# FNet with a gated MLP: MLP blocks of seven units, the first product copied inside PSUM, and x by features for the second half

## The chip, the cores and the metric

The kernel runs on one core of a Trainium2 chip. The metric is the device time of one execution in microseconds (us). Of the kernel before, three runs are given: 821.25, 821.55 and 821.78 us, median 821.55. The engines are named as in the profile: PE (TensorE, matmuls), DVE (VectorE), ACT (ScalarE), POOL (GpSimd) and SP (SyncE, which here issues loads); PEld is PE's loading of weights.

## The reference

The input x has 2048 rows (positions) of 512 features, in float32. What is computed, cut to what matters:

```python
xn = layernorm(x)                                   # over the 512 features
a = einsum("bsd,ed->bse", xn, dft_hid_re)           # 512 x 512
b = einsum("bsd,ed->bse", xn, dft_hid_im)
s = einsum("ts,bse->bte", dft_seq_re, a) - einsum("ts,bse->bte", dft_seq_im, b)   # 2048 x 2048
g = xn @ w_gate                                     # 512 x 1792
u = xn @ w_up
g = silu((sigmoid(g) * u) @ w_down)                 # 1792 x 512
return x + s * g
```

## The kernel before, in words

**Arithmetic.** Every float32 product is made of three matmuls at the lower-precision float32 format of PE: each operand is split into a high part (an ACT copy, line 67) and a low part (a DVE subtraction, line 68), and `mm3` (lines 70 to 73) adds high by high, high by low and low by high into one PSUM bank. On top of that each 2x2 block product is made with seven products instead of eight, so that operands are sums of blocks (`combine`, line 119, on DVE; `x_sum`, line 216, for x) and outputs are sums of products, partly added in PSUM.

**Phases.** (1) `start` opens with the MLP block h=0, g=0 (h: half of the positions, 1024 each; g: one of seven groups of 256 hidden features). There x arrives in tiles of 128 positions, is normalised (`norm_a`, `norm_b`), transposed on PE (`turn`, line 177) and copied out of PSUM (`keep_hi` line 196, `keep_lo` line 202, `keep_raw` line 188); its matmuls (line 555) are 256 columns wide. (2) The blocks h=0, g=1 to 6 and h=1, g=0 come from `block_units`, and h=1, g=1 to 6 from `late_units`. (3) `seq_units` makes the transform over positions: four blocks of positions (`tc_`), seven products, four parts (`pp`) each. (4) `hidden_units` makes the transform over features, multiplies by the gate and writes out.

**An MLP block.** Seven products k of two outputs (gate and up), each of 12 matmuls of 512 columns, gather in three pairs of banks: `ga`/`ua`, `gb`/`ub`, `gc`/`uc`. The order is 1, 2, 6, 5, 7, 4, 3. Product 1 goes to the a banks; `snap` copies it into a page on ACT (line 309 in `block_units`, 473 in `late_units`). Product 2 goes to the b banks, and `plus` adds them to that page on DVE (line 313, 477). Product 6 goes on in the a banks, is snapped, and so on until product 4. The second product of a block's result (`down`, four items of 12 matmuls; in the second half the class `Seven`, seven items of 6) is carried out within the next block. In the first half these items are units of their own:

```python
add(xo(1, 2) + wo(1, 2), u1)
add(bw, lambda: carried(0, 1, 0, 0))
add(xo(6, 5) + wo(6, 5), u3)
add(bw, lambda: carried(1))
```

`gather` (lines 292 to 296) copies their two banks into a page and POOL stores it to `g_part`, adding onto what is there.

**What sets the order.** Nothing is planned by costs. The program is a list `units` of (needs, run), walked at the end; each engine executes in the order in which the program issues. At unit n the walk first runs the hooks that `sooner(n, ...)` left, then issues loads for the units up to n+5, then makes the splits for the units up to n+2, then runs the unit, then runs the hooks of `after(n, ...)`:

```python
for k in range(n, min(n + SPLIT_AHEAD + 1, len(units))):
    for p in units[k][0]:
        p.get()
run()
```

Loads are issued on SP's queue, stores on POOL's; a load waits for the store that it reads. Working memory is 53 pages of 128 x 1024 float32. In `start`, the weights of the first four products of the next block are split while the opening block runs (`units[0 if n < 2 else 2][0][2 + n % 2].get()`: products 1, 2, 6, 5). The outputs of the opening block pass `gated` (line 566 sigmoid on ACT, 567 product on DVE) and `finish` (lines 274 and 275, the split), and after the last of them `x_sum(h, 1)` and `x_sum(h, 2)` are issued.

**Side work** in the h=0 blocks: the tiles 8 to 15 of x (the second half) are fetched, normalised, transposed in four groups of two tiles (eight transposes each) and stored; sums of the transform's operands are made ahead and stored (`t_part`, `s_part`); the sums and splits of x for h=1 are placed around the border of the halves, some before and some after it.

Of the kernel before, what the change touches and what calls it, by code (L numbers as in the profile page):

```python
# [15 lines left out]
P = 128  # L16
# [7 lines left out]
SB = 512  # L24
# [8 lines left out]
def fnet_glu_kernel(ctx: ExitStack, tc: tile.TileContext, x, x_t, c_re, c_im, w_h, w_gu, w_down, out):  # L33
# [22 lines left out]
    nc.scalar.activation(warm, mhalf, AF.Sigmoid)  # L56
    xn_part = dram.tile([2, 2, 2, P, 4, D // 2], F32, name="xn_part")
# [6 lines left out]
    t_part = dram.tile([2, 4, P, 2, SB], F32, name="t_part")  # L64
# [87 lines left out]
    def norm_a(i):  # L152
        st = stat.tile([P, 6], F32, name="st")
        mv = stat.tile([P, 2], F32, name="mv")
        rs = stat.tile([P, 2], F32, name="rs")
        nc.vector.bn_stats(st, xs[i])
        nc.vector.bn_aggr(mv, st)
        nc.gpsimd.tensor_scalar(rs[:, 0:1], mv[:, 1:2], EPS, None, op0=ALU.add)
        nc.gpsimd.tensor_tensor(rs[:, 1:2], rs[:, 0:1], mhalf, op=ALU.pow)
        st_of[i] = mv, rs  # L160

    def norm_b(i):
        mv, rs = st_of.pop(i)
        nc.vector.tensor_scalar(xs[i], xs[i], mv[:, 0:1], rs[:, 1:2], op0=ALU.subtract, op1=ALU.mult)
# [106 lines left out]
    def finish(h, hs, b, f, s):  # L271
        pg = page([2, SB])
        hs[f, b] = pg[:, 0, :], pg[:, 1, :]
        nc.scalar.activation(pg[:, 0, :], s, AF.Copy)
        return lambda: nc.vector.tensor_sub(pg[:, 1, :], s, pg[:, 0, :].bitcast(F32))

    def down(job, n):

        h, g, hs, wd = job
        b, i = divmod(n, 2)  # L280
        for o in range(2):
            at = slice((2 * i + o) * P, (2 * i + o + 1) * P)
            po = bank("pd")
            for f in range(2):
                mm3(po, [t[:, at] for t in wd[f].get()], hs[f, b], f == 0, f == 1)
            yield (2 * h + b) * 2 + i, po

# [10 lines left out]
    def block_units(h, g, before, late, keep=None):  # L298

        w = w_operands(h, g)  # L300
        hs, s, ps = {}, {} if keep is None else keep.s, {}
        wdl = Load(w_down[g], [2, D])
        wd = [Parts([wdl], lambda f=f: wdl.load()[:, f, :], [D], joint=True) for f in range(2)]
        job = (h, g, hs, wd)

        def snap(k, tag):
            s[k] = page([2, SB], F32)
            for m, c in enumerate("gu"):
                nc.scalar.activation(s[k][:, m, :], ps[c + tag], AF.Copy)  # L309

        def plus(k, tag):
            for m, c in enumerate("gu"):
                nc.vector.tensor_add(s[k][:, m, :], s[k][:, m, :], ps[c + tag])
            nc.scalar.activation(s[k][:, 0, :], s[k][:, 0, :], AF.Sigmoid)

        def go(k, tag, first=False):
            for m, c in enumerate("gu"):
                if first:
                    ps[c + tag] = bank(c + tag)
                product(k, ps[c + tag], w, h, m, first)  # L320

        def carried(n, k=None, b=0, f=0):
            outs = list(down(before, n)) if before else []
            if k is not None:
                nc.vector.tensor_mul(s[k][:, 0, :], s[k][:, 0, :], s[k][:, 1, :])
            if outs:
                gather(before[1], outs)
            if k is not None and keep is None:
                finish(h, hs, b, f, s[k][:, 0, :])()

        def u1():
            go(1, "a", True)
            snap(1, "a")
            go(2, "b", True)
            plus(1, "b")

        def u3():
            go(6, "a")
            snap(2, "a")
            go(5, "c", True)  # L340

        def u5():
            go(7, "a")
            snap(3, "a")
            plus(3, "c")

        def u7():
            go(4, "a")
            s[4] = page([2, SB], F32)
            nc.scalar.activation(s[4][:, 0, :], ps["ga"], AF.Sigmoid)  # L350

        def u8():
            go(3, "c")
            nc.vector.tensor_mul(s[4][:, 0, :], s[4][:, 0, :], ps["ua"])
            late = finish(h, hs, 0, 1, s[4][:, 0, :]) if keep is None else lambda: None
            plus(2, "c")
            late()

        n = len(units)
        for i, v in zip((-2, -1, 1, 4), w["s"]):  # L360
            sooner(n + i, v.get)
        if h == 0:
            for i in range(2):
                after(n + 5 * i, lambda i=i: nc.gpsimd.dma_start(ws_part[g, i], w["kept"][i].get()))
        bw = list(before[3]) if before else []
        xo = lambda *k: [xop[h, n] for n in k]
        wo = lambda *k: [w[n] for n in k]
        add(xo(1, 2) + wo(1, 2), u1)
        add(bw, lambda: carried(0, 1, 0, 0))
        if late:  # L370
            add(*late.pop(0))
        add(xo(6, 5) + wo(6, 5), u3)
        if late:
            add(*late.pop(0))
        add(bw, lambda: carried(1))
        add(xo(7) + wo(7), u5)
        add(bw, lambda: carried(2, 3, 1, 1))
        add(xo(4) + wo(4), u7)
        add(xo(3) + wo(3), u8)
        add(bw, lambda: carried(3, 2, 1, 0))  # L380
        if keep:
            keep.spread(len(units) - 7)
        return keep or job


    SEVEN = (2, 1, 6, 7, 4, 5, 3)
    waiting = []

    class Seven:


        def __init__(self, g):
# [71 lines left out]
    def late_units(h, g, before):  # L464

        w = w_operands(h, g)
        job = Seven(g)
        s, ps = job.s, {}
        n = len(units)
        def snap(k, tag):  # L470
            s[k] = page([2, SB], F32)
            for m, c in enumerate("gu"):
                nc.scalar.activation(s[k][:, m, :], ps[c + tag], AF.Copy)

        def plus(k, tag):
            for m, c in enumerate("gu"):
                nc.vector.tensor_add(s[k][:, m, :], s[k][:, m, :], ps[c + tag])

        def gate(k):
            nc.scalar.activation(s[k][:, 0, :], s[k][:, 0, :], AF.Sigmoid)  # L480

        def times(k):
            nc.vector.tensor_mul(s[k][:, 0, :], s[k][:, 0, :], s[k][:, 1, :])

        def last():
            s[4] = page([2, SB], F32)
            nc.scalar.activation(s[4][:, 0, :], ps["ga"], AF.Sigmoid)

        tail = {
            1: lambda: snap(1, "a"),  # L490
            2: lambda: plus(1, "b"),
            6: lambda: snap(2, "a"),
            7: lambda: (snap(3, "a"), plus(3, "c")),
            4: last,
            3: lambda: plus(2, "c"),
        }
        gated = {2: 1, 7: 3, 3: 2}
        CH = {1: "a", 2: "b", 6: "a", 5: "c", 7: "a", 4: "a", 3: "c"}

        def unit(k, d):  # L500
            first = k in (1, 2, 5)
            for m, c in enumerate("gu"):
                tag = c + CH[k]
                if first:
                    ps[tag] = bank(tag)
                product(k, ps[tag], w, h, m, first)
            if k in tail:
                tail[k]()
            if d:
                d[0].run(d[1])  # L510
            if k in gated:
                gate(gated[k])
            if k == 4:
                nc.vector.tensor_mul(s[4][:, 0, :], s[4][:, 0, :], ps["ua"])
# [12 lines left out]
    def start(h, g):  # L527
# [4 lines left out]
        w, hs, ps = {}, {}, {}  # L532
# [11 lines left out]
        def chunk(q, f, order, between=None):  # L544
# [5 lines left out]
            for n, (u, v) in enumerate(order):  # L550
                if n and n - 1 in (between or {}):
                    between[n - 1]()
                for j, m, k in itertools.product(range(2), repeat=3):
# [5 lines left out]
                        start=n == d == 0,  # L559
# [4 lines left out]
        def gated(b, f):  # L564
# [3 lines left out]
            return lambda: finish(h, hs, b, f, s)()  # L568

        def begin():  # L570
# [27 lines left out]
            for p in units[0][0] + units[2][0]:  # L598
                p.load()
# [27 lines left out]
            for q in range(4):  # L627
                for f in range(2):
# [11 lines left out]
                    if 0 <= n < 4:  # L640
                        units[0 if n < 2 else 2][0][2 + n % 2].get()
# [6 lines left out]
        return (h, g, hs, wd), begin  # L648
# [30 lines left out]
    def sums_ahead(n, make, blocks, to, at=(3, 5, 6, 8)):  # L679
# [7 lines left out]
        for i, v in enumerate(blocks):  # L687
            sooner(n + i // 2, v.load)
        for i, v in enumerate(steps):
            after(n + at[i], lambda v=v: step(*v))  # L690
# [36 lines left out]
    def seq_units(job):  # L727
# [8 lines left out]
        for tc_ in range(NT):  # L736
            n = len(units)
            if tc_ == 1:
                blocks = [Load(w_h[i, j], [4, D // 2]) for i in range(2) for j in range(2)]
                sums_ahead(n + 6, diffs, blocks, w_part, (3, 4, 5, 6))  # L740
# [102 lines left out]
            for k in ORDER:  # L843
                for pp in range(4):
                    m = len(units)
                    if (tc_ or pp > 1) and k in bop["t", pp]:
# [115 lines left out]
    with tc.manual_schedule():  # L962
# [3 lines left out]
        for h in range(NH):  # L966
            n = len(units)
            for g in range(NG):
                m = len(units)
                if h and g:  # L970
                    job = late_units(h, g, job)
# [91 lines left out]
```

## Time and profile before

| what | value |
|---|---|
| median of the three runs | 821.55 us |
| the profiled execution's own time | 821.45 us |
| its span (first to last instruction) | 819.7 us |
| mean granted clock of PE | 0.999 |
| PE busy | 810.4 us, 99% |
| DVE busy | 644.7 us, 79% |
| ACT busy | 490.9 us, 60% |
| POOL busy | 144.3 us, 18% |
| HBM traffic | 122.16 MB read, 88.08 MB written |

A group row of the profile reads: line, engine, operation, out<-in by the program's names, out<-in as partitions x elements and type, x count | busy us, mean ns of one | idle time of the engine just before them, and what ended most of it. A row of the timeline reads: start in us from the start of the span, duration, engine, line, operation, out<-in, count, and in brackets the idle time before it and what ended it. A row of the waits reads: engine, what waited, <- what it waited for: us in total, times, longest. A row of the chain reads: start, duration, engine, tile, line, count. "PE ga L71" is the first matmul of `mm3` into the bank `ga`.

### The profile page before, as it was taken

How to read it: one execution, taken by the hardware profiler on the slowest of the kernel's cores; microseconds unless marked ns; L12 is line 12 of the kernel's file. 1: busy time of each engine (PE TensorE's matmuls, PEld its weight loads, DVE VectorE, ACT ScalarE, POOL GpSimd, SP SyncE). 2: the span in 40 equal slices, each digit the busy share in tenths (PEclk: the TensorE clock that was granted, in tenths of full speed). 3: DMA queues.
4: the chain of work that ended last, by engine and by line, in shares of the span. 5: the costliest groups of instructions: out<-in, count | busy, mean ns of one | idle time of the engine just before them, and what ended most of it. 6: DMA issues, size and time to landing. Idle time of an engine off the chain costs nothing.

```text
span 819.7 us, 10476 instructions
## 1 busy us (share of the span) xinstructions
PE 810.4 (99%) x3686; PEld 672.9 (82%) x3686; DVE 644.7 (79%) x816; ACT 490.9 (60%) x762; POOL 144.3 (18%) x214
## 2 busy tenths in 40 slices
PE   8999999999999999999999999999999999999997
PEld 7988888888878888888888888888888888888786
DVE  6798867757788867876797796889888976997956
ACT  4566655655677888887787773444354545535441
POOL 3143432321111122222121100011101110002201
PEclk9999999999999999999999999999999999999999
DMA  8459999799667889989999997358937994789984
GB/s 289 174 176 407 265 267 267 188 320 311 162 170 172 231 177 215 250 203 197 281 292 306 278 336 271 137 203 313 323 136 282 353 384 147 254 317 399 331 254 78
DMA packets 59253, 207.27 MB, mean 253 GB/s; under 512 B 6592, under 2 KB 6848, under 8 KB 59200
## 3 DMA queue, kind: packets, MB, share of 16 engines
q0 software_dynamic: 25072, 87.57, 42.4%
q1 hardware_dynamic: 34128, 119.03, 40.0%
q8 instruction: 29, 0.48, 0.2%
q14 instruction: 24, 0.20, 0.1%
HBM read 122.16 MB, written 88.08 MB: 256 GB/s over the span
## 4 chain that ended last, share of the span: by engine, by line
PE 93%; DVE 3%; ACT 1%; issue 1%; DMA 0%; POOL 0%; SPq 0%; DVEq 0%
PE pd L71 6%; PE pd L72 6%; PE pd L73 6%; PE ga L71 5%; PE ga L72 5%; PE ua L72 5%; PE ga L73 5%; PE ua L71 5%; PE ua L73 5%; PE uc L71 3%; PE gc L72 3%; PE uc L72 3%; PE gc L73 3%; PE gc L71 3%; PE uc L73 3%; PE gb L72 3%
## 5 line engine op out<-in xcount | busy, mean ns | idle before, releaser
L68 DVE TENSOR_TENSOR page<-page 128x1024 fp32r<-128x1024 f32 (+1 forms) x340 | 321.8, 977 | 115.2 <-ACT page L67 113.7
L67 ACT ACTIVATE page<-page 128x1024 fp32r<-128x1024 f32 (+1 forms) x340 | 276.2, 859 | 92.0 <-DVE page L119 72.0
L119 DVE TENSOR_TENSOR page<-page 128x1024 f32<-128x1024 f32 (+2 forms) x184 | 169.0, 933 | 8.5 <-DMA page<-xn_part 6.4
L292 ACT ACTIVATE page<-pd 128x512 f32<-128x512 f32 x154 | 89.4, 595 | 62.2 <-PE pd L73 58.9
L296 POOL DMA_DIRECT2D g_part<-page x69 | 60.1, 882 | 276.2 <-ACT page L292 203.9
L71 PE MATMUL pd<-page 128*128 128x512 f32 x242 | 94.3, 389 | 0.8 <-DVE page L900 0.8
L72 PE MATMUL pd<-page 128*128 128x512 f32 x242 | 94.2, 389 | 0.0
L73 PE MATMUL pd<-page 128*128 128x512 f32 x242 | 94.2, 389 | 0.0
L71 PE MATMUL ga<-page 128*128 128x512 f32 x200 | 78.0, 390 | 0.8 <-ACT page L309 0.8
L73 PE MATMUL ga<-page 128*128 128x512 f32 x200 | 77.9, 389 | 0.0
L72 PE MATMUL ga<-page 128*128 128x512 f32 x200 | 77.9, 389 | 0.0
L73 PE MATMUL ua<-page 128*128 128x512 f32 x200 | 77.8, 389 | 0.0
L72 PE MATMUL ua<-page 128*128 128x512 f32 x200 | 77.8, 389 | 0.0
L71 PE MATMUL ua<-page 128*128 128x512 f32 x200 | 77.8, 389 | 0.0
L71 PEld LDWEIGHTS pd<-page 128*128 128x128 f32 x242 | 45.4, 188 | 10.7 <-issue 1.2
L73 PEld LDWEIGHTS pd<-page 128*128 128x128 f32 x242 | 45.4, 188 | 9.5
L72 PEld LDWEIGHTS pd<-page 128*128 128x128 f32 x242 | 45.4, 188 | 9.3
L71 PE MATMUL ub<-page 128*128 128x512 f32 (+1 forms) x126 | 48.3, 383 | 0.5 <-DVE page L942 0.5
L71 PE MATMUL gc<-page 128*128 128x512 f32 x124 | 48.6, 392 | 0.0
L71 PE MATMUL uc<-page 128*128 128x512 f32 x124 | 48.3, 389 | 0.0
L73 PE MATMUL gc<-page 128*128 128x512 f32 x124 | 48.3, 389 | 0.0
L73 PE MATMUL uc<-page 128*128 128x512 f32 x124 | 48.3, 389 | 0.0
(135 smaller groups left out, 1362.4 us busy)
## 6 DMA issues: line engine op xcount, KB each, us to landing
g_part<-page POOLq DMA_DIRECT2D x77, 512.0 KB, 7.7
page<-in_c_re_dram SPq DMA_DIRECT2D x36, 512.0 KB, 6.2
page<-f_part SPq DMA_DIRECT2D x36, 512.0 KB, 5.6
page<-in_c_im_dram SPq DMA_DIRECT2D x34, 512.0 KB, 6.1
page<-in_w_gu_dram SPq DMA_DIRECT2D x28, 512.0 KB, 7.2
f_part<-page POOLq DMA_DIRECT2D x28, 512.0 KB, 6.4
page<-in_w_down_dram SPq DMA_DIRECT2D x14, 512.0 KB, 8.8
page<-xn_part SPq DMA_DIRECT2D x14, 512.0 KB, 7.8
```

The source lines that it names most:

```text
L67: nc.scalar.activation(hi, src, AF.Copy)
L68: nc.vector.tensor_tensor(lo, src, hi.bitcast(F32), op=SUB)
L71: nc.tensor.matmul(ps, ws[0], ms[0], start=first, stop=False, skip_group_check=go_on)
L72: nc.tensor.matmul(ps, ws[0], ms[1], start=False, stop=False, skip_group_check=go_on)
L73: nc.tensor.matmul(ps, ws[1], ms[0], start=False, stop=last, skip_group_check=go_on)
L119: (engine or nc.vector).tensor_tensor(dst, a, b, op=op)
L292: nc.scalar.activation(pg[:, o, :], po, AF.Copy, scale=float(sign))
L296: nc.gpsimd.dma_start(g_part[i], pg, accum_op=ADD)
```

## The change

1. `block_units` and `late_units` become one function `block`: seven units in the order 1, 5, 2, 6, 7, 4, 3. The down items run inside these units: in the first half (class `Plain`) at the places 1, 3, 4 and 6, in the second half (`Seven`) one at each from the second unit on, as in `late_units`.
2. The first product is not copied into a page. `seed` copies it on ACT from the a banks into the b banks, and product 2 adds onto the copy there; the sigmoid and the product of the gate read the b banks. Two DVE additions of each block go. In `start`, only the first 256 columns' matmul of a bank carries the start flag.
3. The tiles 8 to 15 are no longer transposed. The mean and scale of each position are kept in `moments`, stored to `m_part` in DRAM and loaded back, broadcast to all partitions; the already transposed input x_t is loaded and normalised by features on DVE (eight operations of 128x1024). The normalised rows are still stored for phase 3.
4. Side work has unit numbers of its own. The t sums of pp=1 are no longer made ahead and stored (`t_part` is halved) but made within phase 3, tc_=0. The sums and splits of x for h=1 stand before the border of the halves (only the split for product 7 after it).
5. In `start`, the weights split ahead are those of the units in their new order (1, 5, 2, 6); w_down's two halves are split as one page (`Plain`).

```diff
-        for i, k in enumerate((1, 2, 6, 5, 7, 4, 3)):
+        for i, k in enumerate((1, 5, 2, 6, 7, 4, 3)):
             if i == 1:
-                waiting.extend((before, d) for d in SEVEN)
-            d = waiting.pop(0) if waiting else None
+                waiting.extend((before, d) for d in before.items)
+            d = waiting.pop(0) if waiting and i in waiting[0][0].at else None
...
-            1: lambda: snap(1, "a"),
-            2: lambda: plus(1, "b"),
...
+        def seed():
+            for c in "gu":
+                ps[c + "b"] = bank(c + "b")
+                nc.scalar.activation(ps[c + "b"], ps[c + "a"], AF.Copy)
...
+        tail = {1: seed, 6: lambda: snap(2), 7: lambda: (snap(3), plus(3)), 3: lambda: plus(2)}
+        CH = {1: "a", 5: "c", 2: "b", 6: "a", 7: "a", 4: "a", 3: "c"}
...
-            first = k in (1, 2, 5)
+            first = k in (1, 5)
...
+            if k in (2, 4):
+                gate({2: 1, 4: 4}[k], CH[k])
...
-        sooner(n + 2, lambda: times(1))
+        sooner(n + 3, lambda: times(1, "b"))
...
+    def turned_half(n, b, at):
+        both = Load(m_part[b].rearrange("m t -> (m t)").partition_broadcast(P).rearrange("p (m t) -> p m t", m=2), [2, SB])
+        raw = [Load(x_t[(2 + b) * 2 + j], [2, SB]) for j in range(2)]
+        def store():
+            at = slice(b * SB // P, (b + 1) * SB // P)
+            for m in range(2):
+                nc.gpsimd.dma_start(m_part[b, m].rearrange("(o p) -> p o", p=P), moments[:, m, at])
+        def step(j, m):
+            v = xraw[1, j, b] = raw[j].load()
+            by = both.load()[:, m, :].unsqueeze(1).to_broadcast([P, 2, SB])
+            nc.vector.tensor_tensor(v, v, by, op=(SUB, ALU.mult)[m])
+        after(n, store)
+        for v in (both, *raw):
+            sooner(n + 8, v.load)
+        for i in range(4):
+            after(at[i], lambda i=i: step(*divmod(i, 2)))
...
-            for p in units[0][0] + units[2][0]:
-                p.load()
+            for n in range(4):
+                units[n][0][1].load()
...
-                        units[0 if n < 2 else 2][0][2 + n % 2].get()
+                        units[n][0][1].get()
...
-                if tc_ == 0 and pp < 2:
+                if tc_ == 0 and pp < 1:
...
-                    after(m, lambda i=i: (turn(KH + i), keep_raw(KH + i)))
...
-                for i, k in {-5: 1, -4: 2, 0: 6, 1: 5}.items():
-                    sooner(n + i, xop[1, k].get)
-                for i, k in {-3: 1, -2: 2, 1: 3, 2: 4}.items():
-                    after(n + i, lambda k=k: x_sum(1, k))
+                turned_half(9, 0, (22, 24, 25, 27))
+                turned_half(16, 1, (29, 31, 32, 34))
+                sums_ahead(diffs, xn_blocks(0), s_part[0], (15, 16, 17, 18), 3)
+                sums_ahead(sums, c_blocks(0, 0), t_part[0], (22, 23, 27, 29), 3)
+                sums_ahead(diffs, xn_blocks(1), s_part[1], (49, 55, 56, 62), 3)
+                for i, k in {-6: 1, -5: 2, -3: 3, -2: 4}.items():
+                    after(n + i, lambda k=k: x_sum(1, k))
+                for i, k in {-4: 1, -3: 5, -2: 2, -1: 6, 1: 7}.items():
+                    sooner(n + i, xop[1, k].get)
```

More of the change, by code (lines that the diff above doesn't have):

```diff
@@ L296, in gather @@
             nc.gpsimd.dma_start(g_part[i], pg, accum_op=ADD)
[L298 to L383, printed above, removed]
@@ L485, in last @@
[L485 to L489, printed above, removed]
[L490 to L498 removed]
+                nc.scalar.activation(s[k][:, m, :], ps[c + "a"], AF.Copy)
```

155 lines of the change are left out of this document (91 added, 64 removed).

## The prediction

> **What bounds the kernel now.** I read the busy shares, then the chain that ended last, then the waits of TensorE (PE), and only then the places where PE does wait.
>
> ```profile
> span 819.7 us, 10476 instructions
> PE 810.4 (99%) x3686; PEld 672.9 (82%) x3686; DVE 644.7 (79%) x816; ACT 490.9 (60%) x762; POOL 144.3 (18%) x214
> ...
> PE 93%; DVE 3%; ACT 1%; issue 1%; DMA 0%; POOL 0%; SPq 0%; DVEq 0%
> ```
>
> PE is busy for 99% of the span and carries 93% of the chain. Work taken from another engine therefore gains nothing by itself: only fewer PE slots, or a wait of PE that goes or comes, moves the end. The list of PE's waits is short:
>
> ```profile
> PE gc L575 <- DVE ones L52: 1.4, 1, 1.4
> PE pd L71 <- DVE page L900: 0.8, 1, 0.8
> PE ga L71 <- ACT page L309: 0.8, 1, 0.8
> ```
>
> The first is before all work and the second in the last product of the kernel, and neither is touched. The third is touched (below). To price a PE slot, two rows of PE's timeline with 44 matmuls of 512 columns from the one to the other:
>
> ```profile
> 64.94 0.39 PE L71 MATMUL pd<-page 128*128 128x512 f32 x1
> 74.92 0.39 PE L73 MATMUL pd<-page 128*128 128x512 f32 x1
> ```
>
> 9.98 / 44 = 0.2268 us a slot; the 0.39 is one matmul's own duration, which overlaps the next. Where starts lie further apart than this, PE lost time.
>
> **The change part by part.**
>
> *Transposes of the second half (gone, four groups of eight).* The timeline around one group, and the chain's first and last row of the four:
>
> ```profile
> 61.07 0.40 PE L73 MATMUL ua<-page 128*128 128x512 f32 x1
> 62.41 0.39 PE L72 MATMUL gc<-page 128*128 128x512 f32 x1
> ...
> 61.47 0.87 PE pd L177 x8
> 154.01 0.87 PE pd L177 x8
> ```
>
> Two slots lie between the two matmuls, 0.454 us; the starts are 1.34 apart, so the group costs 1.34 - 0.454 = 0.886, which the chain's 0.87 supports. Four groups: **-3.54 us**. With them go 16 ACT copies; in comes DVE work on x by features, eight operations of 128x1024, at the price of this row, and loads of 512 KB:
>
> ```profile
> L119 DVE TENSOR_TENSOR page<-page 128x1024 f32<-128x1024 f32 x100 | 121.3, 1217 | 8.0 <-DMA page<-xn_part 6.4 <-PE ua L72 1.4
> L313 DVE TENSOR_TENSOR page<-page,gb 128x512 f32<-128x512 f32 x7 | 4.8, 680 | 0.0
> page<-in_w_gu_dram SPq DMA_DIRECT2D x28, 512.0 KB, 7.2
> ```
>
> 8 x 1.217 = 9.7 us of DVE, on an engine that is 79% busy over the span. The adds that the copy in PSUM replaces give room: two of 0.68 in each of 13 blocks, 17.7 us. I cost both at nothing, and would charge 1.2 us for each operation that a split of an operand then waits behind. The loads are issued eight units after the store of the means that one of them reads, 8 x 12 slots x 0.2268 = 21.8 us at the least, against 7.2 for landing. The store has no row of its kind (four bytes at a time); between nothing and the 21.8 us it is hidden. Were it longer, the load would hold SP's queue, and the loads of weights behind it, each issued five units ahead. Nothing for it in the sum. POOL has eight small operations more, at 18% busy: nothing.
>
> *First product copied inside PSUM instead of into a page.* ACT does as many copies as before, of the same 128x512; DVE's adds go; the next product accumulates on the copy. PE's wait becomes that for the copy into gb and ub. In the new order (1, 5, 2, ...) product 5 and, mostly, a down item stand between, at least 12 slots or 2.7 us, against one copy:
>
> ```profile
> L309 ACT ACTIVATE page<-ga 128x512 f32<-128x512 f32 x21 | 12.3, 585 | 1.0 <-PE ga L73 1.0
> L67 ACT ACTIVATE page<-page 128x1024 fp32r<-128x1024 f32 x186 | 188.3, 1054 | 88.7 <-DVE page L119 69.5 <-issue 6.2 <-PE uc L72 5.4
> L68 DVE TENSOR_TENSOR page<-page 128x1024 fp32r<-128x1024 f32 x186 | 222.6, 1220 | 94.2 <-ACT page L67 93.4 <-PE ua L72 0.6
> ```
>
> The copy may stand behind one split of 1.05, giving 1.05 + 2 x 0.585 = 2.2 us, inside 2.7. Nothing; the low end is nothing and the high end is in the third rival.
>
> *The wait at the border of the halves.* Rows of PE, then of ACT:
>
> ```profile
> 227.98 0.39 PE L73 MATMUL pd<-page 128*128 128x512 f32 x1
> 229.13 0.50 PE L71 MATMUL ga<-page 128*128 128x512 f32 x1 [0.76 <-ACT page L309]
> 229.46 0.40 PE L72 MATMUL ga<-page 128*128 128x512 f32 x1
> ...
> 225.56 3.03 ACT L67 ACTIVATE page<-page 128x1024 fp32r<-128x1024 f32 x4
> 228.50 0.57 ACT L309 ACTIVATE page<-ga 128x512 f32<-128x512 f32 x1
> ```
>
> Product 7 waits for the snapshot of ga, which stands on ACT behind four splits of 3.03 us. From 227.98 to 229.46 are two slots, so 1.48 - 0.454 = 1.03 is lost. After the change the sums and the splits of x for the second half are placed at six to one units before the border, one each. ACT then has one, not four splits, ahead of a snapshot: I take **-1.03**; the other end is 0, if they bunch again. What is late next there is PE's own rate.
>
> *Order of the first splits (new wait in the first block).* The opening block splits ahead the weights of the next four products. Second in that order is now product 5, whose operand is a sum made on DVE, where before it was product 2, raw weights. Rows of DVE, ACT and PE of before at that place:
>
> ```profile
> 30.04 0.69 DVE L275 TENSOR_TENSOR page<-page 128x512 fp32r<-128x512 f32 x1 [1.24 <-ACT page L274]
> 30.65 0.68 DVE L68 TENSOR_TENSOR page<-page 128x512 fp32r<-128x512 f32 x1
> ...
> 29.89 0.63 ACT L67 ACTIVATE page<-page 128x512 fp32r<-128x512 f32 x1
> 30.41 0.66 ACT L196 ACTIVATE page<-pd 128x256 fp32r<-128x256 f32 x2
> ...
> 30.85 0.50 PE L555 MATMUL ga<-page 128*128 128x256 f32 x2 [0.64 <-ACT page L196]
> ```
>
> The sum takes the place at 30.65 and ends at 31.33. ACT's split, free to go at 29.89 before, now begins at about 31.36; the copy of tile 7 (L196) stands behind it and starts 0.52 later as it did (29.89 to 30.41), and PE 0.44 after that: 32.32 in place of 30.85, **+1.47 us**. Low end 0 (if the copy had slack, which its 0.64 of PE wait excludes), high end +1.47 plus one more DVE operation, 2.15.
>
> *Product 5 second (new wait behind the first block).* Rows of PE, ACT and DVE:
>
> ```profile
> 36.70 0.40 PE L71 MATMUL ga<-page 128*128 128x512 f32 x1
> ...
> 36.66 0.60 ACT L566 ACTIVATE page<-gb 128x512 f32<-128x512 f32 x1 [0.69 <-PE gb L555]
> 38.01 0.63 ACT L274 ACTIVATE page<-page 128x512 fp32r<-128x512 f32 x1 [0.75 <-DVE page L567]
> ...
> 37.29 0.69 DVE L567 TENSOR_TENSOR page<-page,ub 128x512 f32<-128x512 f32 x1 [0.59 <-ACT page L566]
> 38.67 0.69 DVE L275 TENSOR_TENSOR page<-page 128x512 fp32r<-128x512 f32 x1 [0.70 <-ACT page L274]
> 39.28 2.48 DVE L216 TENSOR_TENSOR page<-page 128x1024 f32<-128x1024 f32 x2
> ```
>
> Product 1 starts at 36.70 and has 12 slots, so product 5 is due at 39.42. It needs the x sum, first of the two operations at 39.28, behind the gate chain of the opening block, in the program of both kernels. The sum ends near 40.5, ACT's split near 41.6, the low part stands behind the second sum (41.76) and ends at 41.76 + 1.22 = 42.98. The first matmul of product 5 wants the high part (2.2 us late), the second, due at 39.65, the low: **+3.33 us**. Before, product 2, a down item and product 6 stood ahead of it, 36 slots or 8.2 us, and covered it; that cover is now behind it. Ends: 2.2 (only the high part late) and 3.6 (the low part behind another half-size operation). After a gap the first step is longer, 229.13 to 229.46, 0.1 over a slot; for three gaps **+0.3**.
>
> *Side work at other units, half of the t sums in the sequence phase.* Four DVE operations of 1.2 us come into the first 28 units of that phase, some 88 us, and four stores and eight loads go. Nothing, if DVE keeps ahead as it does (it waits for nothing there that PE needs sooner than the next unit); 1.2 for each that does not. The sums moved to other units take along their loads on SP and their stores on POOL. In the program order of the changed kernel every load of a page still stands at least 74 slots, 16.8 us, ahead of its first reader, against the 7.2 of a landing: nothing. The split of w_down is one of 1.05 on ACT instead of two halves, three units after the block's first: nothing.
>
> *Sum*, against the profiled run's 821.45 (median 821.55): -3.54 - 1.03 + 1.47 + 3.33 + 0.3 = +0.53, so **822.0 us**. Within 0.2% (1.64 us) a measurement of this kernel can hardly tell a change from none.
>
> **The rivals.** *The clock falls in the new gap (slower).* Rows of PE and of the windows of the end (columns: the window, its length, busy time of five engines, granted clock, DMA share):
>
> ```profile
> 1.45 4.48 PE L575 MATMUL gc<-ones 128*128 128x512 f32 x10 [1.45 <-DVE ones L52]
> ...
> 815.10 0.28 PE L73 MATMUL ub<-page 128*128 128x256 f32 x1
> ...
> 817.00:818.00 1.00, 0.00 (x0) 0.00 (x0) 0.00 (x0) 0.00 (x0) 0.00 (x0) 0.99 0.96 341
> 818.00:819.00 1.00, 0.00 (x0) 0.00 (x0) 0.00 (x0) 0.00 (x0) 0.00 (x0) 0.50 0.01 3
> ```
>
> The ten matmuls at the start lie 0.45 apart, twice a slot, and some 2.6 us after the last matmul ended (815.38) the clock is down to 0.50. The gap before product 5 is 2.2 + 1.1 us with one matmul between. If that suffices, PE runs at half rate until it has been busy for a while. The only such stretch on the trace lasted 4.5 us (1.45 to 5.93); between that and the 2.2 us of the longer gap I take 3.4, of which half is lost: +1.7, **823.7 us** (823.1 to 824.2). It decides from about 2.6 us of idleness in one stretch. The Trainium skill ("TensorE: Matmul & The Clock Gate", Part 1: The HAM clock gate) says that a free-running window of about 3.4 us that is idle halves the clock; read as a wholly idle window, that would spare this gap and leave 822.0. The trace's end, down after 2.6 us, leans the other way.
>
> *Product 5 is not late (faster).* The x sum needs only tiles that were ready near 32; if its place on DVE came ahead of the gate chain, the split would be done by 39.42 and 3.33 + 0.2 fall out: **818.5 us**. For it: the inputs; against: the position in the program.
>
> *Snapshots come too late in the second half.* Products 6 and 7 use one bank; in the second half six blocks now have only 13 slots (2.95 us) between them where there were more. ACT needs 0.585 behind at most two splits of 1.05, 2.7 us; the margin is 0.25. If a third split gets ahead, PE loses about half of the border's wait, 0.5 us, in each of six: 822.0 + 3.0 = **825.0 us**. Against it: before, products 7 and 4 had this distance without a wait.
>
> **How the numbers follow.** As forecast 0.46 (820.4 to 823.2 with the ends of its terms), clock 0.34, product 5 not late 0.13, snapshots 0.07. Range 820.4 to 824.2: the first two cases. Faster than 0.2%: 0.13, the third; slower: nearly all of the clock's and the fourth, 0.40; within: 0.47.
>
> **What would show it.** No L177 groups after 37 us; the wait on the snapshot at 228 gone; a PE wait of 2.1 for the copy of tile 7; then a wait of product 5's first matmuls on ACT's and DVE's split, 3.3 together, near 41 to 44.5; granted clock 1.00 in the windows behind it. Wrong if PE waits in every block on gb or ga, or if the slot is no longer 0.2268.

## The result and the profile after

The changed kernel takes 824.46 us (median of six runs, 823.70 to 826.13) against 821.49 us (six runs, 821.25 to 821.88): a ratio of 1.0038, with a 95% interval of 1.0025 to 1.0051. It is slower by 3.0 us. Forecast were 822.0 us, in a range up to 824.2. The runs also differ among themselves by 2.4 us, where those of the kernel before differ by 0.6. The one profiled execution is the shortest of the six, 823.70 us.

PE's list of waits in the changed kernel (engine, what waited, for what: us in total, times, longest; all `mm3` lines are shifted by two, L71 is now L73):

```profile
PE gc L73 <- ACT page L69: 2.3, 1, 2.3
PE ga L533 <- ACT page L223: 2.1, 1, 2.1
PE gc L558 <- DVE ones L52: 1.4, 1, 1.4
PE pd L73 <- DVE page L883: 0.8, 1, 0.8
PE gc L74 <- DVE page L70: 0.8, 1, 0.8
```

The third and fourth were there before. The snapshot's wait (L309) is gone. The first and fifth are new, and the second has grown from 0.64 us. They are the two waits of the prediction: ga on the copy of tile 7, and product 5 on its high and then its low part. PE's timeline at the three places, and the granted clock behind them (columns of the windows as in the prediction; the last is GB/s):

```profile
32.31 0.50 PE L533 MATMUL ga<-page 128*128 128x256 f32 x2 [2.10 <-ACT page L223]
...
40.69 0.39 PE L75 MATMUL ua<-page 128*128 128x512 f32 x1
43.43 0.50 PE L73 MATMUL gc<-page 128*128 128x512 f32 x1 [2.35 <-ACT page L69]
44.73 0.50 PE L74 MATMUL gc<-page 128*128 128x512 f32 x1 [0.80 <-DVE page L70]
...
45.42 0.63 PE L73 MATMUL gc<-page 128*128 128x512 f32 x1
45.84 0.63 PE L74 MATMUL gc<-page 128*128 128x512 f32 x1
```
```profile
42.00:44.00 2.00, 0.50 (x1) 0.19 (x1) 1.97 (x3) 1.68 (x3) 0.00 (x0) 1.00 0.01 4
44.00:46.00 2.00, 1.27 (x4) 1.03 (x5) 2.00 (x4) 2.00 (x4) 0.00 (x0) 0.79 0.00 0
46.00:48.00 2.00, 2.00 (x7) 1.51 (x6) 2.00 (x2) 0.35 (x1) 0.00 (x0) 0.50 0.55 139
48.00:50.00 2.00, 2.00 (x9) 1.64 (x8) 1.89 (x3) 0.00 (x0) 0.00 (x0) 0.86 0.96 342
```

The first matmul of ga starts at 32.31, where 32.32 was forecast. From 40.69 to 44.73 are 4.04 us for two slots, so 3.59 are lost, where 3.33 was forecast. Then the clock falls to 0.50 and some eight matmuls start 0.43 apart instead of 0.23: about 1.6 us. So the profiled run is the prediction's clock rival, 823.7 us. That it agrees to the tenth is partly luck: the single terms are off by up to 0.4 us each, as shown below. It does not explain the other five runs, which are up to 2.4 us longer.

### The profile page after: what moved, and what is told of

The parts are those of the page before. It is cut to its first block, busy times and chain, and to the rows that moved or that the text cites. A ratio compares the mean times of both kernels' runs of the same rounds, so it can differ in the third digit from the quotient of the medians.

```text
span 821.9 us, 10340 instructions
## 1 busy us (share of the span) xinstructions
PE 808.8 (98%) x3654; PEld 671.5 (82%) x3654; DVE 636.5 (77%) x792; ACT 486.4 (59%) x740; POOL 147.5 (18%) x222
## 4 chain that ended last, share of the span: by engine, by line
PE 94%; DVE 3%; ACT 1%; issue 1%; POOL 0%; DVEq 0%
PE pd L73 6%; PE pd L75 6%; PE pd L74 6%; PE ga L73 5%; PE ua L73 5%; PE ga L74 5%; PE ua L74 5%; PE ua L75 5%; PE ga L75 5%; PE gc L74 3%; PE uc L73 3%; PE gc L75 3%; PE uc L74 3%; PE uc L75 3%; PE gc L73 3%; PE gb L74 3%
## 5 line engine op out<-in xcount | busy, mean ns | idle before, releaser
L70 DVE TENSOR_TENSOR page<-page 128x1024 fp32r<-128x1024 f32 (+1 forms) x362 | 340.5, 969 | 134.4 <-ACT page L69 133.4
L69 ACT ACTIVATE page<-page 128x1024 fp32r<-128x1024 f32 (+1 forms) x362 | 291.4, 853 | 112.1 <-DVE page L121 77.4
L73 PE MATMUL pd<-page 128*128 128x512 f32 x242 | 94.3, 389 | 0.8 <-DVE page L883 0.8
L73 PE MATMUL ga<-page 128*128 128x512 f32 x200 | 78.0, 390 | 0.0
L73 PE MATMUL ua<-page 128*128 128x512 f32 x200 | 77.8, 389 | 0.0
L73 PEld LDWEIGHTS pd<-page 128*128 128x128 f32 x242 | 45.4, 188 | 10.6 <-issue 1.2
L73 PE MATMUL gc<-page 128*128 128x512 f32 x124 | 48.6, 392 | 2.3 <-ACT page L69 2.3
L74 PE MATMUL gc<-page 128*128 128x512 f32 x124 | 48.6, 392 | 0.8 <-DVE page L70 0.8
L73 PE MATMUL ub<-page 128*128 128x512 f32 (+1 forms) x126 | 48.3, 383 | 0.5 <-DVE page L925 0.5
L73 PE MATMUL uc<-page 128*128 128x512 f32 x124 | 48.7, 393 | 0.0
L75 PE MATMUL gc<-page 128*128 128x512 f32 x124 | 48.6, 392 | 0.0
```

Of the source, the lines that this page charges most:

```text
L69: nc.scalar.activation(hi, src, AF.Copy)
L70: nc.vector.tensor_tensor(lo, src, hi.bitcast(F32), op=SUB)
L73: nc.tensor.matmul(ps, ws[0], ms[0], start=first, stop=False, skip_group_check=go_on)
L74: nc.tensor.matmul(ps, ws[0], ms[1], start=False, stop=False, skip_group_check=go_on)
L75: nc.tensor.matmul(ps, ws[1], ms[0], start=False, stop=last, skip_group_check=go_on)
```

## The experiments

**The first block as before.** Of the changed kernel only the block h=0, g=1 gets its old order, and its old snapshot and addition. With the order the weights split ahead in the opening change too: `units[n]` is then product 1, 2, 6, 5 again.

```diff
+        old = (h, g) == (0, 1)
...
+        if old:
+            tail.update({1: lambda: snap(1), 2: plus_b})
...
-        for i, k in enumerate((1, 5, 2, 6, 7, 4, 3)):
+        for i, k in enumerate((1, 2, 6, 5, 7, 4, 3) if old else (1, 5, 2, 6, 7, 4, 3)):
```

> The changed kernel with one part undone: the block h=0, g=1 has the order 1, 2, 6, 5, 7, 4, 3 and the first product's snapshot and addition of the kernel before; all else as changed. Theory (both new waits and the fall of the clock come from product 5 standing second in this one block): both waits and the half-rate matmuls go, and what is left is the four groups of transposes and the wait at the border: 821.5 - 3.5 - 1.0 = 817.0 us (816.6 to 817.4), and the runs lie within 0.6 us of each other as those of the kernel before do. Rival (the seven-unit blocks, the copies in PSUM or the x by features cost time elsewhere): 818 us or more.

Measured: 819.49 us in the median, 818.20 to 823.77 over 12 runs; ratio 0.9987 (0.9973 to 1.0001). The waits near 30 and 43 us are as small as before, yet the time is 2.5 us above 817.0, and spread over 5.6 us. The theory lacked something. PE's timeline of this kernel shows a wait that the profiled run of the changed kernel does not have, with a fall of the clock behind it, and ACT's shows what came late:

```profile
142.90 0.39 PE L75 MATMUL pd<-page 128*128 128x512 f32 x1
145.20 0.50 PE L73 MATMUL ga<-page 128*128 128x512 f32 x1 [1.92 <-ACT page L452]
...
146.75 0.63 PE L73 MATMUL ua<-page 128*128 128x512 f32 x1
147.18 0.63 PE L74 MATMUL ua<-page 128*128 128x512 f32 x1
```
```profile
138.03 0.63 ACT L69 ACTIVATE page<-page 128x512 fp32r<-128x512 f32 x1 [2.27 <-DMA s_part<-page]
...
144.03 0.63 ACT L69 ACTIVATE page<-page 128x512 fp32r<-128x512 f32 x1 [4.88 <-issue]
144.57 0.58 ACT L452 ACTIVATE page<-ga 128x512 f32<-128x512 f32 x1
```

The snapshot L452 stands behind a split (L69). The row gives no releaser for its wait ("issue"); the chain back from the late matmul (start, duration, what) does:

```profile
110.88 15.26 DMA s_part<-page
...
126.42 16.34 DMA xn_part<-page
...
144.03 0.16 ACT page L69
...
144.57 0.59 ACT page L452
...
145.20 0.50 PE ga L73
```

A store of s_part takes 15.26 us to land. POOL's store of rows (xn_part) waits for it and takes 16.34 us, so it lands at 142.75. The split, which needs a free page, begins 1.3 us after that. POOL's timeline shows what was issued around these stores, and the windows (last two columns: DMA share, GB/s) what the DMA engines did meanwhile:

```profile
111.52 1.53 POOL L180 DMA_DIRECT2D m_part<-moments  x2
...
126.42 0.74 POOL L197 DMA_DIRECT2D xn_part<-page  x1 [5.79 <-DMA s_part<-page]
127.86 0.73 POOL L197 DMA_DIRECT2D xn_part<-page  x1 [0.70 <-DMA m_part<-moments]
```
```profile
117.00:122.00 5.00, 5.00 (x23) 4.14 (x23) 5.00 (x8) 3.11 (x6) 1.42 (x2) 1.00 0.99 49
```

Behind the two stores of means and scales (1024 pieces of four bytes, by the program's access pattern) the DMA engines are busy for 99% of five microseconds and move 49 GB/s. These are the stores that the prediction put at nothing. How the small pieces hold the engines up is not shown here, only that they do; the larger pieces below are the test.

**The order of the splits alone, and fillers.** In the first kernel the weights split ahead are taken as 1, 2, 6, 5. In the second, nine matmuls of ones fill the gap ahead of product 5.

```diff
-                        units[n][0][1].get()
+                        units[(0, 2, 3, 1)[n]][0][1].get()
```
```diff
+                if (h, g, k, c) == (0, 1, 5, "g"):
+                    for _ in range(9):
+                        nc.tensor.matmul(ps[tag], ones[:, :P], ones, start=True, stop=True)
                 product(k, ps[tag], w, h, m, first)
```

> The changed kernel, only the weights split ahead in the opening block are taken in the order of products 1, 2, 6, 5. Theory: the wait of the opening block's ga on the copy of tile 7 falls from 2.1 to about 0.6 us, product 5 still waits 3.6 us in two parts, and the clock may fall as before: 824.5 - 1.5 = 823.0 us (822.2 to 824.7, by where the fall of the clock lies). Rival (the wait for product 5 grows by what the first one loses): no change, 824.5.

> The changed kernel with nine matmuls of ones (512 columns, 2.0 us in all) into the bank gc ahead of product 5 in the block h=0, g=1; product 5 starts that bank afresh. They lie inside the gap, so the wait for the splits stays. Theory (the fall of the clock costs 2.0 us in the profiled run and more in others): granted clock 1.00 from 40 to 50 us, no matmul 0.43 apart, 821.9 us (821.5 to 822.4), runs within 0.6 us. Rival (the runs' spread and the rest of the time come from elsewhere): 824 us or more, spread as before.

Measured: 823.93 us (820.27 to 826.15, 12 runs) and 824.28 us (823.12 to 827.55, 6 runs). Both are inconclusive as medians: their profiled runs have the wait on L452 too, near 150 us, of 3.7 and 2.7 us, and the spread covers what was to be seen. Their traces still show what each was for: in the first the wait of ga near 30 us is down to 0.6, and in the second the clock stays at 1.00 from 40 to 48 us. Both were repeated below without the late stores.

**The x sum early.**

```diff
+                    if (q, f) == (3, 0):
+                        x_sum(h, 1)
+                        xop[h, 5].get()
...
             left()
-            x_sum(h, 1)
```

> The changed kernel with the first x sum and its split for product 5 issued ahead of the last gate chain of the opening block. Theory (it is the place on DVE alone that makes product 5 late): product 5 has no wait on the x split. But the last gate chain and the split of w_down come that much later on DVE and ACT, and the first down item, due right behind product 5, now waits about 2 us: 824.5 - 3.7 - 2.0 (clock) + 2.3 = 821.1 us (819.5 to 822.5), the clock at 1.00. Rival (third case of the prediction, nothing is late behind it): 818.5.

Measured: 822.28 us, 821.09 to 825.05 over 12 runs, six of them between 821.09 and 821.49, near the 821.1 that was expected. The profiled run is the longest of the twelve. PE's waits:

```profile
PE ga L73 <- ACT page L452: 2.9, 1, 2.9
PE ga L533 <- ACT page L223: 2.1, 1, 2.1
PE gc L558 <- DVE ones L52: 1.4, 1, 1.4
PE pd L75 <- DVE page L70: 1.2, 1, 1.2
```

Product 5 no longer waits (no row of gc on L69), and the down item behind it does (pd on L70, 1.2): the wait was the place on DVE, and part of it goes on to the next in line. The rival of 818.5, in which nothing behind it is late, is refuted. The trace also holds the longest stretch of the record without a matmul that was not followed by a fall of the clock:

```profile
150.48 0.50 PE L73 MATMUL ga<-page 128*128 128x512 f32 x1 [2.95 <-ACT page L452]
...
150.00:152.00 2.00, 1.52 (x7) 1.26 (x8) 0.67 (x1) 2.00 (x5) 0.00 (x0) 1.00 1.04 336
152.00:154.00 2.00, 2.00 (x10) 1.67 (x9) 1.13 (x1) 2.00 (x4) 1.41 (x2) 1.00 1.07 340
```

**Larger pieces.** Mean and scale of a half of the tiles go out as one transfer of 32 bytes from each partition, 128 pieces in place of 1024; DVE reads the broadcast page with a stride.

```diff
...
-            for m in range(2):
-                nc.gpsimd.dma_start(m_part[b, m].rearrange("(o p) -> p o", p=P), moments[:, m, at])
+            nc.gpsimd.dma_start(m_part[b], moments[:, b].rearrange("p m o -> p (m o)"))
...
-            by = both.load()[:, m, :].unsqueeze(1).to_broadcast([P, 2, SB])
-            nc.vector.tensor_tensor(v, v, by, op=(SUB, ALU.mult)[m])
+            by = both.load().rearrange("p h (q m o) -> p (h q) m o", m=2, o=KH // 2)[:, :, m, :].rearrange("p q o -> p o q")
+            for k in range(2):
+                w = v[:, k, :].rearrange("p (o q) -> p o q", o=KH // 2)
+                nc.vector.tensor_tensor(w, w, by, op=(SUB, ALU.mult)[m])
```

> The kernel f4_first_as_before, with means and scales stored as one transfer of 32 bytes from each partition for each half of the tiles, in place of two transfers of four-byte pieces; the broadcast load then holds them in another order, which DVE reads with a stride (sixteen operations of 128x512 in place of eight of 128x1024). Theory (the four-byte stores fill the DMA engines for some 9 us, the stores behind them land late, pages come free late, ACT's splits wait for a page and PE for the snapshot behind them): no slices of under 100 GB/s at full DMA share near 115 to 126 us, no PE wait on L452 near 143 to 150, 817.0 us (816.6 to 817.6), runs within 0.6 us. Rival (it is the crowding of the side work's pages, whatever the size of the pieces): the wait stays, 818.5 us or more, spread as before.

Measured: 816.90 us (816.66 to 816.93, and one run of 818.22); ratio 0.9946 (0.9934 to 0.9959). The forecast of 817.0 holds, and this version beats both kernels. The same window:

```profile
117.00:122.00 5.00, 5.00 (x24) 4.14 (x23) 5.00 (x7) 3.23 (x6) 2.69 (x5) 1.00 1.06 329
```

329 GB/s in place of 49, and no wait of PE near 145 us. Against this trace the profiled run of the changed kernel loses nothing behind the opening: the same matmul starts 6.61 us later at 102.46 (here 95.85), and the last one 6.64 us later at 817.01 (here 810.37). The same stores alone, in the changed kernel, without and with the fillers:

> The changed kernel with the 32-byte stores alone. Theory: the wait near 145 us goes from all runs, the two waits of the opening and the half-rate matmuls near 45 us stay: 823.6 us (823.0 to 824.0) and the runs within 0.8 us of each other in place of 2.4. Rival (crowding): 824.5, spread as before.

> The kernel h2_m32 with the nine matmuls of ones ahead of product 5 in the block h=0, g=1. With the wait near 145 us away, the price of the clock alone is to be read. Theory (8 matmuls 0.2 us too far apart and four partly so, 2.0 us): 821.6 us (821.2 to 822.2), no matmul 0.43 apart after the opening. Rival (the clock's fall costs nothing on the path): as h2_m32.

Measured: 823.91 us (823.40 to 825.18, 5 runs), and 822.03 us (821.74 to 823.86, 11 runs, six of them at 821.74 to 822.03). The wait near 145 us is gone from the traces of both, but the spread was not down to 0.8 us; the granted clock of these two profiled runs says why. Without fillers:

```profile
32.00:34.00 2.00, 1.95 (x10) 1.95 (x11) 1.12 (x3) 1.12 (x5) 0.00 (x0) 0.63 0.59 223
34.00:36.00 2.00, 2.00 (x11) 2.00 (x11) 0.69 (x1) 0.33 (x1) 0.00 (x0) 0.52 0.03 8
46.00:48.00 2.00, 2.00 (x5) 1.61 (x6) 2.00 (x3) 1.58 (x3) 0.00 (x0) 0.54 0.00 0
48.00:50.00 2.00, 2.00 (x7) 1.52 (x7) 2.00 (x4) 0.00 (x0) 0.00 (x0) 0.61 0.96 290
```

With them:

```profile
32.00:34.00 2.00, 1.37 (x6) 1.37 (x7) 1.36 (x3) 1.12 (x4) 0.00 (x0) 0.62 0.85 262
34.00:36.00 2.00, 2.00 (x12) 2.00 (x11) 0.69 (x1) 0.91 (x3) 0.00 (x0) 0.53 0.03 8
46.00:48.00 2.00, 1.52 (x7) 1.26 (x8) 2.00 (x4) 2.00 (x4) 0.00 (x0) 1.00 0.00 0
```

The clock also falls behind the first gap, of 2.1 us (825.18 is a run with two falls). The fillers take the second fall away while product 5 waits as long: 823.91 - 822.03 = 1.9 us between medians, and 1.7 between the shortest runs.

**The sums moved away from the stores.** `s_part[0]` at the units 36 to 39, with the four-byte stores.

> The kernel f4_first_as_before with its four-byte stores, only the four sums for s_part[0] are made at the units 36 to 39 instead of 15 to 18, so that four pages, loads and stores are away from the four-byte stores of the second half. Theory (four-byte stores): the slices of low GB/s stay; the wait near 145 us gets shorter, since fewer stores stand behind them, but 0.3 to 2 us of it stay in some runs: 817.2 to 819. Rival (crowding alone): the wait is gone from all runs, 817.0 with the low GB/s still there.

Measured: 818.72 us (818.42 to 818.83). The wait near 145 us is gone although the four-byte stores are there (40 GB/s from 117 to 122 us), as the rival had it; a new one of 1.2 us (gc on DVE's L462, near 219 us) has come where the sums went, and with its longer first steps, 1.5 us, it is most of the 1.8 us above 816.9. So both belong to the wait: slow stores, and pages that stand behind them and are wanted soon. Either taken away ends it.

**One part at a time, on the 816.9 us version.** The transposes put back (nobody reads them; the stores of the rows move to the same units), and the splits' order of the changed kernel put back:

```diff
+                        after(b // 7 * 7 + (7, 12 - 7)[b % 7 < 4], lambda j=j: (turn(KH + j), store_xn(KH + j)))
```
```diff
+                        units[(0, 3, 1, 2)[n]][0][1].get()
```

> The kernel h1_first_and_m32 (816.9) with the 32 transposes of the tiles 8 to 15 put back on PE, in four groups of eight at units without a down item; nobody reads them. Theory (a group costs PE 0.886 us and nothing else): 816.9 + 3.5 = 820.4 us (820.1 to 820.8). Rival (the transposes were partly hidden in the weight loads or cost through their copies on ACT): 819 or less.

> The kernel h1_first_and_m32 with the weights split ahead in the order of products 1, 5, 2, 6, so that only the first new wait of the change is in. Theory: the wait of ga on the copy of tile 7 is 2.1 us in place of 0.6, and that alone, 1.47 us, without a fall of the clock: 818.4 us; in the runs where the clock falls after these 2.1 us, 1.2 to 1.7 more: 819.5 to 820.1. Both kinds of runs are expected, since the gap of 2.1 us made the clock fall in some of the traces and not in others. Rival (a gap of 2.1 us never brings the clock down by itself): 818.4 in all runs.

Measured: 820.82 us (820.58 to 820.98), so 3.9 for the transposes, and 819.85 us (818.89 to 820.38) in two groups: five runs at 818.89 to 819.02, six at 819.85 to 820.38. The lower group is 2.1 above 816.9, not 1.47; in its trace 1.47 is the wait of ga (again 2.1 in place of 0.6), some 0.2 are longer steps near 43 us, and 0.3 lie behind the last matmul. The upper group is 1.2 us longer, at a mean granted clock of 0.997 to 0.998 in place of 0.999 to 1.000. That this is a fall behind the gap of 2.1 us is read from the clock; the profiled run is of the lower group.

The other new wait alone, product 5's:

> The kernel h2_m32 with the weights split ahead in the order of products 1, 2, 6, 5: of the two new waits of the opening, only product 5's is left (2.0 and 0.8 us with one matmul between). Theory: without a fall of the clock 816.9 + 3.6 = 820.5 us, with it 1.7 to 2.0 more, 822.4; both kinds of runs, since the same gap was followed by a granted clock of 1.00 in one trace (f2_splits_order) and of 0.50 in others. Rival (the first gap has to come with it for the clock to fall): 820.5 in all runs.

Measured: 821.76 us (820.14 to 823.06): one run of 820.14 at a mean clock of 0.999, seven from 821.16 to 821.98 at 0.996 to 0.997, three from 822.86 to 823.06 at 0.995. So the same program pays nothing, about 1.5 or about 2.8 us, by the clock for the fall. The gap near 30 us is not needed for it.

**The border of the halves.** First, in the kernel before, the x sums and splits of the second half moved ahead of the border, one at a time:

```diff
-                for i, k in {-5: 1, -4: 2, 0: 6, 1: 5}.items():
+                for i, k in {-5: 1, -4: 2, -2: 6, -1: 5, 1: 7}.items():
...
-                for i, k in {-3: 1, -2: 2, 1: 3, 2: 4}.items():
+                for i, k in {-7: 1, -6: 2, -4: 3, -3: 4}.items():
```

> The kernel before, with the sums and splits of x for the second half at seven to one units ahead of the border of the halves, one at a time, as the change has them (only the split for product 7 after it). Theory: the wait of ga for the snapshot at 228 us (0.76, with its longer first steps 1.03 to 1.1 in all) goes and nothing takes its place: 821.5 - 1.05 = 820.4 us (820.2 to 820.7). Rival (they bunch with the down items' copies there): 821.5.

Measured: 822.34 us (822.00 to 822.62), ratio 1.0010 (1.0001 to 1.0019): no gain, but a loss of 0.9 us. The wait is still there; the rows of ACT show what the snapshot of ga now stands behind:

```profile
228.66 0.39 PE L73 MATMUL pd<-page 128*128 128x512 f32 x1
229.85 0.50 PE L71 MATMUL ga<-page 128*128 128x512 f32 x1 [0.80 <-ACT page L309]
...
227.64 0.63 ACT L274 ACTIVATE page<-page 128x512 fp32r<-128x512 f32 x1 [1.69 <-DVE page L325]
228.18 1.13 ACT L67 ACTIVATE page<-page 128x512 fp32r<-128x512 f32 x2
229.22 0.57 ACT L309 ACTIVATE page<-ga 128x512 f32<-128x512 f32 x1
```

Two half-size splits of 1.13 us stand there, not four of 3.03, and the snapshot is as late. Ahead of them is a copy of `finish` (L274) that waits for a product on DVE (L325), 1.69 us here. The kernel before has the same copy ahead of its four splits:

```profile
225.03 0.63 ACT L274 ACTIVATE page<-page 128x512 fp32r<-128x512 f32 x1 [2.10 <-DVE page L325]
```

So the four splits alone were not the cause.

Then the reverse, on the 816.9 us version: the x sums back at the border and the splits left to the look-ahead.

```diff
-                for i, k in {-6: 1, -5: 2, -3: 3, -2: 4}.items():
+                for i, k in {-3: 1, -2: 2, 1: 3, 2: 4}.items():
...
-                for i, k in {-4: 1, -3: 5, -2: 2, -1: 6, 1: 7}.items():
+                for i, k in {-4: 1}.items():
```

> The kernel h1_first_and_m32 with the sums of x for the second half back at three units before to two after the border, and the splits left to the look-ahead of two units, as in the kernel before. Theory, new since h7_before_early_x (the wait at the border goes by the order 1, 5, 2: the snapshot's reader of ga now stands 36 slots and more behind product 1, where 24 were, so ACT may be late): no wait of ga or gb near 220 to 230 us of over 0.2, 816.9 us (816.6 to 817.4). Rival (the prediction's reason: the early splits of x took it away): a wait of about 0.8 there, 817.9 us.

Measured: 817.27 us (817.09 to 817.67), with no wait of ga or gb at the border. It is 0.4 above 816.9, but in the two profiled runs PE is 0.4 us apart by 19 us and no more than that behind the border. In the new blocks the copy of the first product is not late, wherever the x work stands:

```profile
218.05 2.09 ACT L69 ACTIVATE page<-page 128x512 fp32r<-128x512 f32 x3
220.04 0.59 ACT L459 ACTIVATE gb<-ga 128x512 f32<-128x512 f32 x1
220.56 0.55 ACT L459 ACTIVATE ub<-ua 128x512 f32<-128x512 f32 x1
...
225.00 0.39 PE L73 MATMUL gb<-page 128*128 128x512 f32 x1
```

It is done at 221.1, 3.9 us ahead of its first reader, product 2. That reader stands 24 slots behind product 1, as product 6 did before, so it is not the distance that grew: the copy comes earlier on ACT. Which part of the new blocks brings that (the order, one product to a unit, the place of `finish`) was not taken apart.

**Later splits in the opening block**, an attempt at more on the 816.9 us version:

```diff
-                    n = 2 * q + f - 3
+                    n = {(1, 1): 0, (2, 1): 1, (3, 0): 2, (3, 1): 3}.get((q, f), -1)
```

> The kernel h1_first_and_m32, with the second, third and fourth split of weights in the opening block one chunk later each, so that none stands on ACT ahead of the copy of tile 7. Theory (that copy waits behind one split, 0.52 us from its start to the copy's): the wait of ga at 30 us falls from 0.64 to about 0.1 us: 816.4 us (816.2 to 816.7). Rival (the copy waits for PE's transposes or DVE anyway): no change, 816.9.

Measured: 817.76 us (817.72 to 817.90), 0.9 slower than 816.9. The wait of ga near 30 us falls to 0.13, and the first down item then waits 0.68 for the low part of w_down, which the later work on DVE has pushed back.

## Why the prediction was wrong, point by point

- *Transposes, -3.54.* Right to 0.4: putting them back costs 3.9 us.
- *Store of the means, "nothing for it in the sum".* This step failed. I asked only whether its own reader comes late. It lands in 9.2 to 14.3 us in the changed kernel (9.7 to 15.9 with the first block as before), inside the 21.8, so that was no trouble; what I left out is what shares the DMA engines with it. Stores beside and behind it land late, their pages come free late, ACT's split waits for one, and PE for the snapshot behind. That cost the first-block-as-before kernel 2.6 us in the median (819.49 against 816.90) and made its spread. In the profiled run of the changed kernel it was seen only on ACT (row below): a split waits 2.7 us for a store, and PE is not held up. In the three kernels that differ from it only in the opening (order of the splits, fillers, x sum early) PE is held up, by 3.7, 2.7 and 2.9 us. What lengthened the other five runs is not shown by a trace of them. The larger pieces take 0.55 us off the median (824.46 to 823.91), but 823.40 to 825.18 lies mostly inside the old spread. The mean clocks point to two causes: the runs of 824.92 and 825.43 us have 0.995, close to the 0.994 of the kernel with larger pieces in its two long runs, of which the traced one has two falls; the run of 826.13 us has 0.997, as the profiled one, so there a wait such as L452's is more likely.

```profile
146.33 0.63 ACT L69 ACTIVATE page<-page 128x512 fp32r<-128x512 f32 x1 [2.72 <-DMA xn_part<-page]
```

- *Copy inside PSUM, nothing.* Right: no row of PE waiting for the copy.
- *The border, -1.03.* Right in size, for the wrong reason and with the wrong product: it is product 6, not 7, that waits there for product 1's snapshot. The prediction's reason, the early x splits, is refuted by both border runs. That the wait goes with the new blocks is shown; which part of them does it stays open. So it was luck that the term came out.
- *Order of the first splits, +1.47.* Right to 0.01 us in the profile; alone, on the 816.9 us version, it cost 2.1 us in the time, or 3.3 with a fall of the clock.
- *Product 5 second, +3.33 and +0.3.* Measured 3.59 and a longer step of 0.1 behind it, against 3.33 and two of the three longer steps: right to 0.2.
- *No fall of the clock, chance 0.46.* This step failed, and it is the largest: the sum put the fall of the clock at nothing. It came in the profiled run, by the mean clock (0.995 to 0.997, where the runs of the kernel before have 0.998 to 1.000) in all six runs of the changed kernel, and by clock and times in ten of the eleven runs that have product 5's gap alone. The price I set, 1.7, was good (about 1.6 in the trace, 1.7 to 1.9 by the fillers). The point from which it decides was wrong: not 2.6 us in one stretch. The clock fell after 1.92 us (first block as before, 145 us) and after 2.1 us, and did not after 2.95 us (x sum early, 150 us), so length alone does not decide.
- *Snapshots in the second half, chance 0.07.* Did not come: no such row.

The Trainium skill ("TensorE: Matmul & The Clock Gate", Part 1: The HAM clock gate) gives an idle window of about 3.4 us as the condition. Read as a wholly idle stretch, these traces differ: the shortest before a fall was 1.92 us. They are in keeping with its free-running window, since one and the same gap brings the clock down in some runs and not in others.

With the clock's fall my sum would have been 823.7, the profiled run. The median lies 0.8 above it and 0.26 above the range: the range's upper end had the fall in it, but neither a second fall nor the stores. Three of the six runs (823.70 to 824.00) are inside the range and three (824.92 to 826.13) are not, and the median is the middle between them; how the two causes share in the three is open.

## What to carry to other kernels

Price a transfer by its pieces as well as its bytes, and ask what else uses the DMA engines beside and behind it: 4 KB in pieces of four bytes held up stores of 256 and 512 KB, and with them the pages that PE's suppliers needed some 30 us later. Count an idle gap of PE of two microseconds at its length and at a likely 1.2 to 2 us of half-rate matmuls behind it, and put filler matmuls there if it can't go. When an order is changed inside repeated blocks, walk the first block by itself: its operands are made late, and it held both new waits, while in the blocks behind it PE shows no wait for the new order.

## What the runs showed of the hardware that was not expected

Two transfers of 1024 four-byte pieces in all kept the DMA engines at a share of 0.99 with 49 GB/s moved (117 to 122 us); as 128 pieces of 32 bytes the same data left 329 GB/s in that window. The Trainium skill ("DMA: Bandwidth & Descriptors", Specifications) asks for 512 bytes at the least for the full rate; both sizes lie below it, and only the first hurt here.

The clock fell after as little as 1.92 us without a matmul, stayed at about 0.5 for some 3 us, and did so after one and the same gap of 2.1 us in six of eleven runs of one program (by their times and mean clock). After 2.95 us in another trace it did not fall. Times of such a program fall in groups, so a median over a few runs says less than the groups do.
